# Scaling both halves of q on VectorE in the first seven pairs of a fused retention and WaveMLP kernel

## The chip, the cores and the metric

The kernel runs on one core of one Trainium2 chip. The metric is the device time of one execution in microseconds (us). The kernel before takes 168.33 us (median of 3 runs, 168.14 to 168.94). PE is TensorE, DVE is VectorE, ACT is ScalarE, POOL is GpSimd, SP is SyncE, which only issues transfers here. A run counts as slow when it lies more than 1.5% above the fastest run of its kernel; ratios use the other runs, called fast.

## The reference, cut to what matters

```python
# retention over q, k, v of shape (4, 8, 768, 64), fp32
for t in range(S):
    state = gamma * state + outer(k[:, :, t], v[:, :, t])
    y[:, :, t] = scale * (q[:, :, t] @ state)
x = y.transpose(0, 2, 1, 3).reshape(B, S, H * D)
# WaveMLP phase
theta = x @ w_theta
y = w_tok_r @ (x * cos(theta)) + w_tok_i @ (x * sin(theta))   # over tokens
u = x + y
out = u + relu(u @ w_ch)
```

The kernel works in blocks. It multiplies q by `scale * gamma**t` and v by `gamma**-t` per token and head; then the decay drops out of the products, and only a causal mask is left.

## The kernel before

The work goes in 12 "pairs" (three per batch), each with two 128-token blocks of q, k and v. A pair's q is 512 KB of fp32. `prep` scales it and casts it to bf16, in two halves of 128x512:

```python
def prep(n, name, engines):
    t = work.tile([P, 2, dm], BF, name="kqb", bufs=12)
    ...
    sc = qscp if name == "q" else vscp
    for two in range(2):
        engines[two].tensor_mul(dst[:, two], src[:, two],
                                _bcast_last(sc[:, 2 * g + two], D))
```

In pairs 0 to 6 `engines` for q is `DP = (DV, PL)`, one half on DVE and one on POOL; v is always on POOL (`PP`). Later pairs have both on POOL. TensorE then transposes the scaled q and k into a PSUM tile of the tag "tr" (two buffers), which DVE copies to SBUF:

```python
def flip(n, name, copy=nc.vector.tensor_copy):
    ps = psum.tile([P, 2, NP, P], BF, name="kq_ps", tag="tr", bufs=2)
    ... # eight nc.tensor.transpose
    copy(t, ps)
```

The same two buffers serve the transposes of the token weights (`w_ps`), of x (`x_ps`) and the channel product (`o_ps`), so each waits until DVE or ACT has emptied the tile before it (in pair 6 DVE's copy of x ended at 63.46 us and the transposes of q began at 63.50). `x_sb` is the copy of x's transposes, `z` is x times cos and sin, `at` is the masked block product. Pair 6's part of the program, on each engine in this order:

```python
# iteration n = 5, cut
ret_mask(n, 0)                       # DVE: at
prep(n + 1, "k", (PL,))              # POOL: k of pair 6
preps(DP)                            # q: DVE and POOL; v: POOL
...
theta(n - 1, 0); x_pe(n - 1)         # PE, then DVE: x_sb
theta(n - 1, 1)
flip(n + 1, "k"); flip(n + 1, "q")   # PE, then DVE: kqT
```

Of the kernel before, what the change touches and what calls it, by code (L numbers as in the profile page):

```python
# [21 lines left out]
def _bcast_last(ap: bass.AP, n: int) -> bass.AP:  # L22
    return bass.AP(tensor=ap.tensor, offset=ap.offset, ap=list(ap.ap) + [[0, n]])
# [9 lines left out]
def kernel(  # L33
# [42 lines left out]
    def load(n, name):  # L76

        b, g = divmod(n, nG)
        t = io.tile([P, H, 2 * D], FT, name="pair", bufs=7)
        src = dict(k=k, q=q, v=v)[name]  # L80
        nc.sync.dma_start(out=t, in_=src[b, :, 2 * g * P:2 * (g + 1) * P, :].rearrange(
            "h (p two) d -> p h (two d)", two=2))
        raw[n, name] = t
# [78 lines left out]
    def prep(n, name, engines):  # L162
        g = n % nG
        t = work.tile([P, 2, dm], BF, name="kqb", bufs=12)
        src = raw[n, name].rearrange("p h (two d) -> p two h d", two=2)
        dst = t.rearrange("p two (h d) -> p two h d", h=H)
        if name == "k":
            if engines[0] is nc.scalar:
                nc.scalar.copy(dst, src)
            else:  # L170
                engines[0].tensor_copy(dst, src)
        else:
# [4 lines that stand above are left out]
        st[n, name] = t  # L177
# [4 lines that stand above are left out]
            for j in range(NP):  # L182
                nc.tensor.transpose(ps[:, two, j, :],  # L183
                                    st[n, name][:, two, j * P:(j + 1) * P], ident)
        t = work.tile([P, 2, NP, P], BF, name="kqT", bufs=6)
        if copy:
            copy(t, ps)  # L187
        st[n, name + "T"], st[n, name + "_ps"] = t, ps

    def flip_out(n, name):  # L190
        nc.vector.tensor_copy(st[n, name + "T"], st[n, name + "_ps"])

    def flip_dma(n, name):
        t = work.tile([P, 2, NP, P], BF, name="kqT", bufs=6)
        nc.sync.dma_start_transpose(out=t.rearrange("p w j t -> p (w j) t"),
                                    in_=st[n, name].rearrange("p w d -> p (w d)"))
        st[n, name + "T"] = t
# [111 lines left out]
    def theta(n, a):  # L309
        th_ps = psum.tile([P, dm], FT, name="th_ps", tag="acc", bufs=2)  # L310
        for j in range(NP):
            nc.tensor.matmul(th_ps, st[n, "xT"][:, a, j, :], wth[:, j, :], start=(j == 0),  # L312
                             stop=(j == NP - 1))
        cs = work.tile([P, 2, dm], BF, name="cs", bufs=3)
        nc.scalar.activation(cs[:, 0, :], th_ps, AF.Sin, bias=halfpi, scale=1.0)  # L315
        nc.scalar.activation(cs[:, 1, :], th_ps, AF.Sin, bias=zerob, scale=1.0)  # L316
        st[n, "cs", a] = cs
# [32 lines left out]
    def moe_U_dma(m):  # L350
        uT = work.tile([P, nD, P], BF, name="uT", bufs=4)
        nc.sync.dma_start_transpose(out=uT, in_=mo[m]["u"])
        mo[m]["uT"] = uT
# [30 lines left out]
    def w_cast(t0):  # L384
        for r in range(2):
            row = work.tile([P, S], BF, name="wrow", bufs=5)
            nc.gpsimd.tensor_copy(row, wdma[r, t0])  # L387
            wrow[r, t0] = row
# [73 lines left out]
    def keep_busy(times):  # L462
        for _ in range(times):
            nc.tensor.matmul(warm_ps, warm[:, 0:P], warm, start=True, stop=True)


    DV, PL, AC = nc.vector, nc.gpsimd, nc.scalar
    DP, PP = (DV, PL), (PL, PL)
    keep_busy(12)
    prep(0, "k", (AC,))  # L470
    flip(0, "k", None)
    prep(0, "q", DP)
    flip_out(0, "k")
    keep_busy(3)
    flip(0, "q")
# [18 lines left out]
    ret_out(0, 0, DV.tensor_copy)  # L494
    ret_out(0, 1, DV.tensor_copy)
    keep_busy(3)
    prep(1, "q", DP)
    theta(0, 0)
    flip(1, "k")
    theta(0, 1)  # L500
# [22 lines left out]
    prep(2, "k", (PL,))  # L523
    zmul(0, 0)
    flip(2, "k")
    prep(2, "q", DP)
    theta(1, 0)
    zmul(0, 1)
    theta(1, 1)
# [26 lines left out]
    moe_M(0, 2, 3)  # L556
    theta(2, 0)
    flip(3, "k")
    prep(3, "q", DP)
    theta(2, 1)  # L560
    moe_M(0, 3, 4)
    x_pe(2)
# [29 lines left out]
    for n in range(nG, B * nG + 1):  # L592
        mine, done = tiles_of[n], tiles_of[n - 1]
        late, two = n > nG, len(mine) > 1
        nxt = n + 1 in pairs

        if nxt and n + 1 >= K_DMA:
            flip_dma(n + 1, "k")
        if nxt and n + 1 >= Q_DMA:
            flip_dma(n + 1, "q")  # L600
        if n <= X_DMA and n + 3 in pairs:
            load(n + 3, "k")
        if n >= U_DMA:
            moe_U_dma(done[1])
        def preps(engines):
            prep(n + 1, "q", engines)
            prep(n + 1, "v", PP)
            if n in (nG, nG + 1):
                w_cast(n - nG + 4)

        if n == nG:
            nc.gpsimd.tensor_copy(wch, wdma["ch"])
        if nG + 3 < n + 1 < Q_DMA:
            preps(PP)
        if late:
            ret_I(n - 1, 1)

        if n in pairs:
            ret_A(n, 0)
            ret_mask(n, 0)  # L620
        if n == nG:
            moe_M(0, 5, nT)
            w_flip(1, 2)
            moe_u(0)
            moe_M(1, 4, nT)
            moe_u(1)
        if late:
            ret_Y(n - 1, 1)
            ret_S(n - 1, 1)
            ret_out(n - 1, 0, nc.scalar.copy)  # L630
            ret_out(n - 1, 1, nc.scalar.copy)
            state_out(n - 1, 1)
            if n < nG + 3:
                prep(n + 1, "k", (PL,))
                if n > nG + 1:
                    preps(DP)
            if n - 1 >= X_DMA:
                x_dma(n - 1)
        if n > X_DMA and n + 3 in pairs:
            load(n + 3, "k")  # L640
        if n + 3 in pairs:
            load(n + 3, "q")

        first = mine[0]
        moe_M(first, 0, 3 if two else 2)
        if late:
            theta(n - 1, 0)
            if n - 1 < X_DMA:
                x_pe(n - 1)
            if n == nG + 1:  # L650
                preps(DP)
            theta(n - 1, 1)
        if two:
            moe_M(first, 3, nT)
            moe_u(first)
        for name, limit in (("k", K_DMA), ("q", Q_DMA)):
            if nxt and nG + 1 < n + 1 < limit and (n > nG + 1 or name == "k"):
                flip(n + 1, name)
        if n + 1 >= K_DMA and not two:
            moe_M(first, 2, 4)  # L660
        if n + 3 in pairs:
            load(n + 3, "v")
        for t in stores_in(n):
            store(t)
        if n + 1 >= U_DMA:
            moe_U_dma(first)

        if n in pairs:
            ret_S(n, 0)
            state_out(n, 0)  # L670
            ret_A(n, 1)
            ret_mask(n, 1)
            ret_Y(n, 0)
            ret_I(n, 0)
        if n < U_DMA:
            moe_U(done)
        if n == nG:
            prep(n + 1, "k", (AC,))
            preps(DP)
        if n == nG or n + 1 < K_DMA and not two:  # L680
            moe_M(first, 2, 4)
        early_z = late and n < nG + 3
        if early_z and n > nG + 1:
            zmul(n - 1, 0)
        if n < nG + 3:
            w_tok(n - nG + 3)
        if early_z:
            zmul(n - 1, 0 if n == nG + 1 else 1)
        if not two:
            moe_M(first, 4, nT)  # L690
            if n == nG + 1:
                flip(n + 1, "q")
            moe_u(first)
            if n == nG + 1:
                zmul(n - 1, 1)
        elif n in pairs:
            moe_M(mine[1], 0, nT)
        if n + 2 in pairs and n > nG + 1:
            prep(n + 2, "k", (AC,))
        if n + 2 in pairs and n + 2 >= Q_DMA:  # L700
            prep(n + 2, "q", PP)
            prep(n + 2, "v", PP)
        if two and n in pairs:
            moe_u(mine[1])
        for i, t in enumerate(done):
            if n == nG:
                flip(n + 1, "kq"[i])
            moe_O(t)
            moe_out(t)
        if late and not early_z:  # L710
            zmul(n - 1, 0)
            zmul(n - 1, 1)
        if n not in pairs:
            moe_M(mine[1], 0, nT)
            moe_u(mine[1])
# [43 lines left out]
```

## Time and profile before

| | busy us | share of the 166.5 us span |
|---|---|---|
| PE | 155.2 | 93% |
| DVE | 102.4 | 61% |
| ACT | 79.1 | 48% |
| POOL | 66.6 | 40% |

A busy share is an average over stages with different limits. From 70 us on TensorE hardly waits (it is busy for 9.84 of the 10 us from 70 to 80 and 31.74 of the 32 from 100 to 132); from 30 to 70 us its waits are short (38.30 of 40 us busy). So the views to read are the timelines of DVE and POOL up to 70 us and the chain of waits there.

### The profile page before, as it was taken

To read this page: it belongs to the slowest core of one execution; us is meant where nothing else is said; L and a number is where in the kernel's file an instruction comes from. 1 tells how busy PE (TensorE), PEld (TensorE's weight loads), DVE (VectorE), ACT (ScalarE), POOL (GpSimd) and SP (SyncE) were. 2 spreads that over 40 slices of the span, in tenths; PEclk is the share of its full clock that TensorE was granted. 3 is DMA by queue.
4 is the path that set the end of the run, shared out by engine and by line. 5 is a ranking of instruction groups with operands and counts; after the bars stand their busy time and mean duration, and the time that the engine had idled before them with its cause. 6 is when DMAs were issued, how large, how long until landed. Compare 5 with 4: busy or idle time off the path is not lost.

```text
span 166.5 us, 4614 instructions
## 1 busy us (share of the span) xinstructions
PE 155.2 (93%) x1933; PEld 87.2 (52%) x1959; DVE 102.4 (61%) x137; ACT 79.1 (48%) x137; POOL 66.6 (40%) x82
## 2 busy tenths in 40 slices
PE   6969897899999999999999999999999999999991
PEld 2345664664755667555555554455545444444460
DVE  2257798878686699939446464584554736334442
ACT  7216568371819467687847827447083350000010
POOL 6275959786685877771442703600000000000000
PEclk9999999999999999999999999999999999999999
DMA  4999999999999999999999999998996161753343
GB/s 122 309 345 307 326 326 354 286 328 317 293 311 349 277 278 331 309 202 250 206 231 298 163 242 203 195 233 168 266 145 185 32 189 32 231 115 100 106 141 135
DMA packets 68901, 38.45 MB, mean 231 GB/s; under 512 B 26256, under 2 KB 63376, under 8 KB 68880
## 3 DMA queue, kind: packets, MB, share of 16 engines
q1 hardware_dynamic: 68736, 38.02, 90.2%
q8 instruction: 15, 0.25, 0.7%
q10 hardware_dynamic: 144, 0.13, 0.2%
q14 instruction: 6, 0.05, 0.1%
HBM read 25.69 MB, written 6.29 MB: 192 GB/s over the span
## 4 chain that ended last, share of the span: by engine, by line
PE 77%; DVE 12%; DMA 3%; issue 3%; ACT 1%; POOL 1%; DVEq 0%; SPq 0%; POOLq 0%
PE y_ps L340 33%; PE o_ps L368 12%; PE th_ps L312 11%; PE at_ps L208 4%; PE yT_ps L231 4%; DVE at L215 4%; DMA pair<-in_q_dram 3%; PE yT_ps L245 3%; PE st_ps L262 3%; PE kq_ps L183 3%; DVE z L322 2%; PE w_ps L393 2%; DVE kqT L187 2%; PE y_ps L420 2%; DVE kqb L175 1%
## 5 line engine op out<-in xcount | busy, mean ns | idle before, releaser
L340 PE MATMUL y_ps<-z,wtr 128*128 128x512 bf16 x133 | 50.5, 379 | 1.1
L340 PE MATMUL y_ps<-z,wti 128*128 128x512 bf16 x122 | 46.2, 379 | 0.4 <-issue 0.2
L347 DVE TENSOR_TENSOR u<-y_ps,x_sb 128x512 bf16<-128x512 f32 x23 | 15.9, 690 | 27.0 <-PE y_ps L340 27.0
L215 DVE TENSOR_TENSOR at<-at_ps,maskp 128x1024 bf16<-128x1024 f32 x24 | 29.3, 1221 | 4.6 <-PE at_ps L208 4.6
L175 POOL TENSOR_TENSOR kqb<-pair,qscp 128x512 bf16<-128x512 f32 x17 | 19.3, 1150 | 28.9 <-DMA pair<-in_q_dram 26.0
L175 POOL TENSOR_TENSOR kqb<-pair,vscp 128x512 bf16<-128x512 f32 x24 | 26.6, 1131 | 5.0 <-DMA pair<-in_v_dram 4.9
L285 ACT CAST xT<-yT_ps 128x512 bf16<-128x512 f32 x20 | 13.5, 739 | 30.0 <-PE yT_ps L231 29.9
L375 DVE SCALAR_TENSOR_TENSOR ot<-o_ps,u 128x512 f32<-128x512 f32 x23 | 15.9, 690 | 13.2 <-PE o_ps L368 13.2
L312 PE MATMUL th_ps<-wth,xT 128*128 128x512 bf16 x93 | 23.2, 379 | 0.5 <-ACT xT L285 0.3
L368 PE MATMUL o_ps<-wch,uT 128*128 128x512 bf16 x92 | 22.8, 379 | 0.3
L340 PEld LDWEIGHTS <-wtr 128*128 128x128 bf16 x138 | 13.5, 98 | 13.8
L276 ACT CAST stbd<-st_ps 64x256 bf16<-64x256 f32 x40 | 14.7, 368 | 12.5 <-PE st_ps L262 12.0
L340 PEld LDWEIGHTS <-wti 128*128 128x128 bf16 x138 | 13.5, 98 | 13.6 <-ACT wti L400 0.4
L315 ACT ACTIVATE cs<-th_ps,halfpi 128x512 bf16<-128x512 f32 x24 | 16.5, 689 | 7.0 <-PE th_ps L312 6.6
L322 DVE TENSOR_TENSOR z<-cs,x_sb 128x1024 bf16<-128x1024 bf16 x24 | 18.8, 808 | 0.1
L316 ACT ACTIVATE cs<-th_ps,zerob 128x512 bf16<-128x512 f32 x24 | 16.5, 687 | 0.0
L312 PEld LDWEIGHTS <-xT 128*128 128x128 bf16 x96 | 8.9, 98 | 11.0 <-ACT xT L285 1.0
L368 PEld LDWEIGHTS <-uT 128*128 128x128 bf16 x92 | 8.8, 98 | 10.5 <-issue 0.6
L208 PE MATMUL at_ps<-kqT 64*64 64x128 bf16 x384 | 10.6, 221 | 2.6 <-DVE at L215 1.8
L430 ACT COPY uT<-u_ps 128x384 bf16<-128x384 bf16 (+1 forms) x2 | 0.7, 372 | 25.5 <-PE u_ps L429 25.5
L187 DVE COPY kqT<-kq_ps 128x1024 bf16<-128x1024 bf16 x14 | 9.6, 688 | 4.2 <-PE kq_ps L183 4.1
L387 POOL CAST wrow<-wtok 128x768 bf16<-128x768 f32 x12 | 10.5, 902 | 0.3 <-DMA wtok<-in_moe_w_tok_i_dram 0.2
(61 smaller groups left out, 164.4 us busy)
## 6 DMA issues: line engine op xcount, KB each, us to landing
pair<-in_k_dram SPq DMA_DIRECT2D x12, 512.0 KB, 6.7
pair<-in_q_dram SPq DMA_DIRECT2D x12, 512.0 KB, 7.7
pair<-in_v_dram SPq DMA_DIRECT2D x12, 512.0 KB, 8.2
out_dram<-ot SPq DMA_DIRECT2D x23, 256.0 KB, 2.6
wtok<-in_moe_w_tok_r_dram SPq DMA_DIRECT2D x6, 384.0 KB, 6.4
wtok<-in_moe_w_tok_i_dram SPq DMA_DIRECT2D x6, 384.0 KB, 5.8
w<-in_moe_w_theta_dram SPq DMA_DIRECT2D x1, 1024.0 KB, 8.3
w<-in_moe_w_ch_dram SPq DMA_DIRECT2D x1, 1024.0 KB, 8.5
```

The source lines that it names most:

```text
L175: engines[two].tensor_mul(dst[:, two], src[:, two], _bcast_last(sc[:, 2 * g + two], D))
L208: nc.tensor.matmul(at_ps[half, par, j, :], kT[rows, two, j, half], qT[rows, :, j, half], start=(j == 0), stop=(j == NP - 1), skip_group_ch ...
L215: nc.vector.tensor_mul(at.rearrange("p a j t -> p (a j) t"), at_ps.rearrange("p a j t -> p (a j) t"), _bcast_mid(maskp[:, two].rearrange(" ...
L276: nc.scalar.copy(stbd[(c + 1) % 2][sl, :, sl], st_ps[b][sl])
L312: nc.tensor.matmul(th_ps, st[n, "xT"][:, a, j, :], wth[:, j, :], start=(j == 0), stop=(j == NP - 1))
L315: nc.scalar.activation(cs[:, 0, :], th_ps, AF.Sin, bias=halfpi, scale=1.0)
L316: nc.scalar.activation(cs[:, 1, :], th_ps, AF.Sin, bias=zerob, scale=1.0)
L322: nc.vector.tensor_mul(zs[b][:, c], st[n, "cs", a], _bcast_mid(xs[b][:, c, :], 2))
L340: nc.tensor.matmul(y_ps, wT[r][:, s0, t0 * P:(t0 + 1) * P], zs[b][:, s0, r, :], start=(s0 == 0 and r == 0), stop=(s0 == nT - 1 and r == 1))
L347: nc.vector.tensor_add(u, mo[m]["y"], xs[b][:, t0, :])
L368: nc.tensor.matmul(o_ps, mo[m]["uT"][:, j, :], wch[:, j, :], start=(j == 0), stop=(j == nD - 1))
L375: nc.vector.scalar_tensor_tensor(ot, mo[m]["o"], 0.0, mo[m]["u"], ALU.max, ALU.add)
```

## The change

The intent is to take the slower engine out of q: POOL needs 1.04 us for a half, DVE 0.69, and each tensor of a pair then belongs to one engine.

```diff
-    DP, PP = (DV, PL), (PL, PL)
+    DD, PP = (DV, DV), (PL, PL)
...
-    prep(0, "q", DP)
+    prep(0, "q", DD)
... (the same for pairs 1, 2, 3)
-                    preps(DP)
+                    preps(DD)
... (the same at the two other places, pairs 4 and 5)
```

More of the change, by code (lines that the diff above doesn't have):

```diff
@@ L496 @@
     keep_busy(3)
-    prep(1, "q", DP)
+    prep(1, "q", DD)
     theta(0, 0)
@@ L525 @@
     flip(2, "k")
-    prep(2, "q", DP)
+    prep(2, "q", DD)
     theta(1, 0)
@@ L558 @@
     flip(3, "k")
-    prep(3, "q", DP)
+    prep(3, "q", DD)
     theta(2, 1)
@@ L650 @@
             if n == nG + 1:
-                preps(DP)
+                preps(DD)
             theta(n - 1, 1)
@@ L678 @@
             prep(n + 1, "k", (AC,))
-            preps(DP)
+            preps(DD)
         if n == nG or n + 1 < K_DMA and not two:
```

## The prediction

> **What bounds the kernel now.** I read the page's busy shares first, then the chain that ended last, then the timelines of VectorE (DVE) and GpSimd (POOL) in the first 70 us, where the changed instructions stand.
>
> ```profile
> span 166.5 us, 4614 instructions
> PE 155.2 (93%) x1933; PEld 87.2 (52%) x1959; DVE 102.4 (61%) x137; ACT 79.1 (48%) x137; POOL 66.6 (40%) x82
> PE 77%; DVE 12%; DMA 3%; issue 3%; ACT 1%; POOL 1%; DVEq 0%; SPq 0%; POOLq 0%
> ```
>
> TensorE is busy 93% of the span and is 77% of the chain, so the end moves only if TensorE waits more or less. DVE has 12% of the chain; POOL, from which the change takes work, has 1%. A table of engine busy time by stretches gives where the waits lie: TensorE works 9.84 of the 10 us from 70 to 80, 19.79 of the 20 us from 80 to 100 and 31.74 of the 32 us from 100 to 132. A delay made before 70 us is therefore not absorbed afterwards. From 30 to 70 us TensorE has 38.3 of 40 us, so little is hidden there either. Before 30 us both DMA arrivals and short chains between engines set the pace.
>
> The groups of instructions give the cost of one scaling of half a pair of q:
>
> ```profile
> L175 POOL TENSOR_TENSOR kqb<-pair,qscp 128x512 bf16<-128x512 f32 x17 | 19.3, 1150 | 28.9 <-DMA pair<-in_q_dram 26.0
> L175 DVE TENSOR_TENSOR kqb<-pair,qscp 128x512 bf16<-128x512 f32 x7 | 5.7, 813 | 5.5 <-DMA pair<-in_q_dram 5.5
> ```
>
> The means hide waiting: the view of the tile gives 1042/1044/1550 ns (least, median, most) on POOL and 668/691/1347 on DVE. Undisturbed, one takes 1.04 us on POOL and 0.69 on DVE, and DVE's next instruction starts 0.61 after it.
>
> [...] These are timelines of POOL and DVE about pair 6, then about pair 2:
>
> ```profile
> 61.26 2.49 POOL L175 TENSOR_TENSOR kqb<-pair,vscp 128x512 bf16<-128x512 f32 x2 [0.51 <-DMA pair<-in_v_dram]
> 61.50 1.35 DVE L175 TENSOR_TENSOR kqb<-pair,qscp 128x512 bf16<-128x512 f32 x1
> ...
> 24.33 0.93 DVE L175 TENSOR_TENSOR kqb<-pair,qscp 128x512 bf16<-128x512 f32 x1
> 25.14 2.49 POOL L175 TENSOR_TENSOR kqb<-pair,vscp 128x512 bf16<-128x512 f32 x2 [0.42 <-DMA pair<-in_v_dram]
> 25.19 1.54 DVE L322 TENSOR_TENSOR z<-cs,x_sb 128x1024 bf16<-128x1024 bf16 x1
> ```
>
> At 61.26 POOL begins the first half of v; DVE's q waits to about 62.30 and then needs 0.55, ending at 62.85; POOL's second half starts only then (1.04 + 0.41 waiting + 1.04 = 2.49). So the two take turns: at 62.30 POOL's own next instruction was ready, and DVE still got its turn; at 25.2 POOL, waiting since 25.14, came before DVE's next instruction z, which then took 1.54. [...]
>
> **The change, part by part.** Seven POOL instructions go (7 x 1.04 = 7.3 us of POOL time, plus its waits) and seven DVE instructions come (7 x 0.61 = 4.3 us of DVE time). The order of the other instructions on every engine is the same. POOL mostly gains nothing on the path: its next work, v, starts after "DMA pair<-in_v_dram" in most pairs. So the freed POOL time becomes idle time. What counts is where DVE's extra 0.61 falls, and whether it makes q take another turn behind v. By pair:
>
> Pair 0: q lands at 7.08. Now POOL's half waits for DVE's and ends at 8.67. With both on DVE the second ends near 8.37. DVE's following copy of k moves to 8.30–8.91, so the copy of q starts at 8.91 in place of 9.16: a gain of 0.25. It lasts until pair 2, whose k cast on POOL waits for DMA until 21.86.
>
> Pair 1: q lands at about 15.2, both halves end near 16.5; TensorE flips q at about 17, so no change.
>
> Pair 2: q halves at 24.1 and 24.7, ending 25.3. v lands at 25.14, so POOL goes next, to 26.35, and z ends at 26.9 in place of 26.7. I take +0.15 on the path.
>
> Pair 3: q begins near 34.43 (34.28 plus 0.15) and v lands at 34.52, in the middle of it. POOL takes the turn, 35.0 to 36.0, and the second q ends at 36.55. Then come the copy of x, 36.5 where it was 35.42, which frees the PSUM buffer for the flip of q, and z behind v's second half, to 38.1 where it was 37.4. That is about +0.65, up to +0.8 with the casts of w behind it.
>
> Pair 4: q lands at 44.09; DVE's copy of w (44.70 now) moves by 0.6 to 0.7, and TensorE's flip of k waits for it with no slack. This coincides with the delay there already: still about +0.8.
>
> Pair 5: DVE sits idle 1.23 us before the copy of w at 56.32, which takes up most of the extra: +0.
>
> Pair 6 decides, as the chain of waits by time shows:
>
> ```profile
> 60.45 1.13 DVE at L215
> 61.58 1.27 DVE kqb L175
> 62.85 0.61 DVE x_sb L306
> 63.46 0.04 issue
> 63.50 0.61 PE kq_ps L183 x8
> ```
>
> Here DVE itself is the path. The copy of x stands behind q on DVE, and TensorE's transposes of q wait for it. With two q instructions the turns are: v to 62.30, q to 62.85, v to 63.90, q to 64.45. If DVE comes later than 62.30 (by the +0.8), both halves of v go first and the second q ends at 64.45 again. So the copy of x starts at 64.45 in place of 62.8, 0.55 + 1.04 = 1.6 later, and the transposes at 65.1 in place of 63.5. The earlier +0.8 lies within these 1.6 and is not added.
>
> [...] TensorE waits for the copy of w behind it (67.44 to 67.97). The shifted order may win back about 0.2 of this. The sum is +1.6 - 0.2 = +1.4 us, to 168.33 + 1.4 = about 169.8.
>
> **The rivals.**
>
> 1. Taking POOL out of q ends the collisions within q and so gains. For it: q took 1.52 and 1.55 on POOL in pairs 0 and 1, with 0.5 of waiting; the two halves now run one after the other anyway (0.55 + 1.04 = 1.6 us, against 1.2 for two on DVE). Against it: only pair 0 has q on the path early enough; the later ones trade a collision of q with q for one of q with v. If the turns favour the engine that is already running, so that two DVE instructions go together, pair 6 costs only 0.6 and pairs 2 and 3 about nothing: 168.0 to 168.9.
>
> 2. The delays add up. If DVE reaches pair 3 some 0.1 us later than I say, POOL's first half of v goes before the first q: then q ends at 37.7 and the transposes of q start about 1.8 late. DVE would then meet v again in pair 4 (45.6), and the delay would come to 2.6 or 3.2 us: 171 to 171.5. The margin (34.43 against 34.52) is too thin to rule it out. Against it: [...] a late DVE finds pair 6's v already done.
>
> 3. The extra DVE time is hidden: DVE is only 61% busy, and 4.3 us more makes 64%. For it: pairs 1 and 5. Against it: the windows 60 to 65 and 65 to 70 have DVE busy 4.99 and 5.00 of 5 us. Fully hidden would mean 168.1 to 168.5.
>
> **Range and chances.** Rival 1 or 3 gives the low end; rival 2 the high end. Between the two the turns of pair 6 are the best supported, by the trace's own order of turns. I take 169.8, with 168.5 to 171.3. A change of 2% is 3.37 us: faster needs below 164.96, more than every gain listed together, so 0.01; slower needs above 171.70, only with rival 2 at its worst, so 0.07; within 2%: 0.92.
>
> **What would show it.** In the changed profile: POOL falls by 7 to 10 us, DVE rises by about 4 to 6 (waits count as busy); in pair 6 the two q instructions span about 2.9 us from 61.5 with v's second half between; the copy of x starts near 64.4 and the transposes of q near 65.1; every TensorE stretch after 70 us is the old one moved by 1.2 to 1.7 us. Wrong would be: the copy of x before 63.6 (turns not alternating), transposes of pair 3's q later than 37.8 (delays adding up), or a later stretch of TensorE that shrinks.

## The result, and the profile after

The first four runs of the changed kernel took 170.39, 174.55, 170.51 and 173.60 us; the second and fourth count as slow. A ratio in this text is the mean time of one kernel's fast runs over that of the other's of the same rounds, so it is not quite the ratio of the medians quoted. The ratio to before is 1.0118 (95% interval 1.0075 to 1.0161): within 2%, on the slow side. The predicted ratio was 169.8/168.33 = 1.0087.

From the page of the changed kernel (span, busy times, chain, the two groups of q):

```profile
span 168.7 us, 4613 instructions
PE 154.6 (92%) x1933; PEld 87.1 (52%) x1959; DVE 106.8 (63%) x144; ACT 79.1 (47%) x137; POOL 57.8 (34%) x75
PE 67%; DMA 11%; SPq 7%; DVE 7%; ACT 2%; issue 2%; POOL 1%; DVEq 0%
L175 POOL TENSOR_TENSOR kqb<-pair,qscp 128x512 bf16<-128x512 f32 x10 | 10.4, 1061 | 20.5 <-DMA pair<-in_q_dram 20.5
L175 DVE TENSOR_TENSOR kqb<-pair,qscp 128x512 bf16<-128x512 f32 x14 | 10.7, 803 | 5.4 <-DMA pair<-in_q_dram 5.3
```

POOL lost 8.8 us of busy time (66.6 to 57.8) and DVE gained 4.4. POOL's relief bought nothing: it became waiting for transfers (4.9 us for v's before, 23.2 after). TensorE's busy time did not grow (155.2 us before, 154.6 after), so the 2.2 us that the span grew are TensorE's waits. Pair 6, the timelines of POOL and DVE:

```profile
61.88 2.05 POOL L175 TENSOR_TENSOR kqb<-pair,vscp 128x512 bf16<-128x512 f32 x2 [1.82 <-DMA pair<-in_v_dram]
63.01 2.07 DVE L175 TENSOR_TENSOR kqb<-pair,qscp 128x512 bf16<-128x512 f32 x2
65.00 0.68 DVE L306 COPY x_sb<-x_ps 128x1024 bf16<-128x1024 bf16 x1
```

and the chain of waits there (start, us, what):

```profile
61.96 1.13 DVE at L215
63.09 1.99 DVE kqb L175 x2
65.08 0.61 DVE x_sb L306
65.69 0.04 issue
65.73 0.61 PE kq_ps L183 x8
```

The chain has the same members as before, but DVE came to q at 63.01 in place of 61.50. The first half of v ended near 62.92 and the second was already running, so both halves of q waited until about 63.9 and then took 1.1 to 1.2 us. The copy of x starts 2.23 us later than before and TensorE's transposes 2.23 later (65.73 against 63.50).

So DVE was 1.5 us late before pair 6. The beginning of that is at pair 2, again DVE and POOL:

```profile
24.37 1.28 DVE L175 TENSOR_TENSOR kqb<-pair,qscp 128x512 bf16<-128x512 f32 x2
25.27 2.73 POOL L175 TENSOR_TENSOR kqb<-pair,vscp 128x512 bf16<-128x512 f32 x2 [2.23 <-DMA pair<-in_v_dram]
25.57 1.53 DVE L322 TENSOR_TENSOR z<-cs,x_sb 128x1024 bf16<-128x1024 bf16 x1
```

The second half of q runs while v is waiting; v goes next, and z waits for it and ends at 27.1.

How late is TensorE after each step? The kernel before was profiled twice and the changed one three times (the further runs are told below). The table has the start of the same TensorE instructions (the last line: DVE's first output of the last tile) in the timelines, and in brackets the lateness against the mean of the two profiles of before.

| instruction | before, twice | after | after_again | after_third |
|---|---|---|---|---|
| products of pair 2 (at_ps) | 27.38, 27.27 | 27.76 (+0.43) | 27.73 (+0.40) | 27.84 (+0.51) |
| transposes of pair 3's q | 36.41, 36.32 | 37.06 (+0.69) | 36.77 (+0.40) | 36.88 (+0.51) |
| products of pair 3, second block | 41.73, 41.63 | 42.80 (+1.12) | 42.09 (+0.41) | 42.26 (+0.58) |
| transposes of pair 4's k | 45.30, 45.19 | 46.81 (+1.56) | 46.09 (+0.84) | 46.26 (+1.01) |
| transposes of pair 5's q | 57.32, 57.22 | 58.82 (+1.55) | 58.32 (+1.05) | 58.28 (+1.01) |
| products of pair 6 | 69.14, 68.61 | 71.12 (+2.24) | 69.98 (+1.10) | 70.23 (+1.35) |
| first output of the last tile | 162.81, 162.28 | 164.79 (+2.24) | 163.65 (+1.10) | 163.90 (+1.35) |

Three steps recur: about 0.4 to 0.5 us at pair 2, another 0.43 to 0.44 from pair 3's second block to pair 4's k, and 0.05 to 0.7 about pair 6. Pair 3 itself added 0.7 in the first profile and at most 0.1 in the others. The two profiles of before differ by 0.43 us in what passes at pair 6, so the last step is uncertain by some 0.2. After pair 6 nothing is lost or won back.

In pair 4 DVE's copy of the weights stands behind q, as predicted, but a second thing came with it. From the timelines of ACT, DVE and PE in the second profile of the changed kernel:

```profile
44.14 1.29 DVE L175 TENSOR_TENSOR kqb<-pair,qscp 128x512 bf16<-128x512 f32 x2 [0.29 <-DMA pair<-in_q_dram]
45.24 0.80 ACT L400 COPY wti<-w_ps 128x768 bf16<-128x768 bf16 x1
45.35 0.55 DVE L400 COPY wtr<-w_ps 128x768 bf16<-128x768 bf16 x1
46.09 0.61 PE L183 MATMUL kq_ps<-ident,kqb 128*128 128x128 bf16 x8 [0.29 <-ACT wti L400]
```

In the kernel before the transposes of k followed DVE's copy (44.70 to 45.25, transposes 45.30). In the changed one they waited for ACT's copy (46.04): the build gave them the other buffer of "tr", the one that ACT's copy empties. DVE's copy ended at 45.90, so I estimate from these times that without this exchange of buffers they could have started some 0.15 us earlier here, and DVE's later copy would have made the other 0.3 of the step.

All the profiles together put the step down to the exchange. From the products of pair 3's second block to these transposes 3.55 to 3.57 us pass in the six profiles of before, only6, early6_only, pp6 and pp36 (the runs are told below). They are 4.00 to 4.01 in the seven profiles of the kernels with more DVE work in pair 4: the changed one (three profiles), not6, memset_all, merged_all and merged_again. All seven show the wait for ACT's copy. (only01 has 4.21 without it: its q landed late, and the wait was for DVE's copy.) In merged_again DVE's copy had ended at 45.76, well before the transposes (DVE, ACT, PE), so there the exchange alone made the step:

```profile
45.21 0.55 DVE L403 COPY wtr<-w_ps 128x768 bf16<-128x768 bf16 x1
45.35 0.80 ACT L403 COPY wti<-w_ps 128x768 bf16<-128x768 bf16 x1
46.20 0.61 PE L186 MATMUL kq_ps<-ident,kqb 128*128 128x128 bf16 x8 [0.29 <-ACT wti L403]
```

No run changes the exchange and nothing else.

### The profile page after: what moved, and what is told of

It reads as the page before. It is cut to its first block, busy times and chain, and to the rows that moved or that the text cites. A ratio compares the mean times of both kernels' runs of the same rounds, so it can differ in the third digit from the quotient of the medians.

```text
span 168.7 us, 4613 instructions
## 1 busy us (share of the span) xinstructions
PE 154.6 (92%) x1933; PEld 87.1 (52%) x1959; DVE 106.8 (63%) x144; ACT 79.1 (47%) x137; POOL 57.8 (34%) x75
## 4 chain that ended last, share of the span: by engine, by line
PE 67%; DMA 11%; SPq 7%; DVE 7%; ACT 2%; issue 2%; POOL 1%; DVEq 0%
PE y_ps L340 32%; PE o_ps L368 12%; PE th_ps L312 8%; DMA pair<-in_q_dram 6%; SPq L81 5%; DMA pair<-in_k_dram 5%; PE yT_ps L231 3%; PE at_ps L208 2%; PE st_ps L262 2%; PE yT_ps L245 2%; DVE kqb L175 2%; PE kq_ps L183 2%; PE y_ps L420 2%; DVE z L322 1%; SPq L95 1%
## 5 line engine op out<-in xcount | busy, mean ns | idle before, releaser
L175 POOL TENSOR_TENSOR kqb<-pair,vscp 128x512 bf16<-128x512 f32 x24 | 26.7, 1135 | 23.9 <-DMA pair<-in_v_dram 23.2
L347 DVE TENSOR_TENSOR u<-y_ps,x_sb 128x512 bf16<-128x512 f32 x23 | 15.9, 690 | 26.9 <-PE y_ps L340 26.7
L312 PE MATMUL th_ps<-wth,xT 128*128 128x512 bf16 x93 | 23.2, 379 | 0.5 <-ACT xT L285 0.3
L175 POOL TENSOR_TENSOR kqb<-pair,qscp 128x512 bf16<-128x512 f32 x10 | 10.4, 1061 | 20.5 <-DMA pair<-in_q_dram 20.5
L175 DVE TENSOR_TENSOR kqb<-pair,qscp 128x512 bf16<-128x512 f32 x14 | 10.7, 803 | 5.4 <-DMA pair<-in_q_dram 5.3
L183 PE MATMUL kq_ps<-ident,kqb 128*128 128x128 bf16 x120 | 9.3, 219 | 3.0 <-DVE x_sb L306 0.8
```

What stands on the lines that cost most here:

```text
L175: engines[two].tensor_mul(dst[:, two], src[:, two], _bcast_last(sc[:, 2 * g + two], D))
L312: nc.tensor.matmul(th_ps, st[n, "xT"][:, a, j, :], wth[:, j, :], start=(j == 0), stop=(j == NP - 1))
L347: nc.vector.tensor_add(u, mo[m]["y"], xs[b][:, t0, :])
```

## The experiments

All runs gave the right result. "before" was timed in the same rounds. The first four ran on one chip, the next four and the last four likewise.

**before_again** is the kernel before, unchanged, for a second profile.

> The kernel before, profiled a second time, to see how far the landing of transfers differs between two executions. In the first profile q of pair 3 had landed by 32.99 us and its v at 34.52; in the changed kernel they landed at 35.11 and 36.84. If that is chance between executions, this second profile of the same kernel should show landings that differ by 1 us or more from the first; if it belongs to the change, they should agree within 0.3 us. Time about 168.4 us.

One run, 167.68 us. v of pair 3 began at 35.25 (34.52 in the first profile), k of pair 2 at 22.14 (21.86), and v and q of pair 6 had landed by 60.72 and 59.12 (61.26 and 59.36). So the landings of one kernel, that is the ends of its transfers, differ by 0.3 to 0.7 us between these two executions, less than the 1 us that I had named for chance but more than the 0.3 for none. Among the three profiles of the changed kernel v of pair 3, waited for each time, began at 35.36, 36.30 and 36.84: 1.5 us apart. What matters for the argument: which instructions of DVE and POOL meet differs from run to run. In this run z of pair 2 went before v (25.31, 0.68 us; in the first profile it took 1.54 behind v) and TensorE was not late. And at pair 6 TensorE did not wait for DVE (DVE, then PE):

```profile
62.23 0.68 DVE L306 COPY x_sb<-x_ps 128x1024 bf16<-128x1024 bf16 x1
62.72 1.06 PE L183 MATMUL kq_ps<-ident,kqb 128*128 128x128 bf16 x16
```

These are the transposes of k and q in one run; in the first profile they took 1.29 us from 62.81, with the wait for the copy of x in the middle. So the prediction's premise, that DVE is the path in pair 6, held in the first profile and not in this one.

**after_again** is the changed kernel, unchanged.

> The changed kernel again, profiled a second time. Fast runs at about 170.4 us, ratio 1.012. If the late landing of pair 3's q (35.11 us) was chance, it lands nearer 33 us now, DVE meets v in pair 3 in turns (second q ends near 36.5) and the delay of TensorE after pair 3 is still 0.7 to 1.1 us; if it belongs to the change, it lands near 35 again. In either case the copy of x of pair 6 starts 1.6 to 2.3 us later than 62.77 and TensorE stays 1.4 to 2.1 us late to the end.

Fast runs 169.22, 169.41, 169.74 and 170.59 us, two slow ones (173.07, 174.34), ratio 1.0079 (1.0040 to 1.0118). Pair 3's q began at 34.64 without a wait for its transfer, while it began at 35.11 in the first profile of the changed kernel and in not6 below, and at 35.05 in only01 below, whose pair 3 is as before. So the later landing doesn't need the edit of pair 3. Whether those of pairs 0 and 1 bring it is open: three of the seven profiles of kernels that have them show it, and none of the seven without (there POOL began pair 3's q by 33.63). Its cost does belong to the change. In only01, with a half of q on each engine, the copy of x began at 35.66 and TensorE was 0.1 us late after pair 3. In the first profile of the changed kernel the second half of q held that copy until 36.33, z then met v (37.11, 1.32 us), and TensorE lost 0.7. The halves of q of pair 3 ended near 35.9, not in turns with v. Pair 5 did take turns; POOL first, then DVE:

```profile
53.03 2.49 POOL L175 TENSOR_TENSOR kqb<-pair,vscp 128x512 bf16<-128x512 f32 x2 [2.05 <-DMA pair<-in_v_dram]
53.34 2.73 DVE L175 TENSOR_TENSOR kqb<-pair,qscp 128x512 bf16<-128x512 f32 x2
```

v to 54.07, q to 54.6, v to 55.5, q to 56.07: four halves, by turns, 2.73 us for a work of 1.29. It delayed TensorE by only 0.2 us, since DVE had idle time behind it (1.23 us before 56.32 in the first profile of before). (In the first profile pair 5 went q, v, q, v, from 54.05 to 56.18.) The copy of x of pair 6 started at 63.86, 1.1 us later than in the first profile of before, less than I had expected.

**only6** has the change in pair 6 alone.

```diff
                 if n > nG + 1:
-                    preps(DP)
+                    preps(DD)
```

> Only pair 6 has both halves of q on DVE. Turn-taking theory: v's first half to 62.3, first q to 62.85, v's second half to 63.9, second q to 64.45, so the copy of x starts near 64.4 in place of 62.8, and the kernel takes 1.2 to 1.6 us more: 169.5 to 170.0 us, ratio 1.007 to 1.010. Rival, only DVE's time counts (0.61): 168.9 to 169.0, ratio 1.003 to 1.004. Rival, the lateness of pairs 2 to 5 is what counts: 168.3, ratio 1.000.

Ratio 1.0051 (1.0019 to 1.0083), median 169.10 us; six fast runs. Its timelines of POOL and DVE:

```profile
60.70 2.52 POOL L175 TENSOR_TENSOR kqb<-pair,vscp 128x512 bf16<-128x512 f32 x2 [2.07 <-DMA pair<-in_v_dram]
61.64 2.13 DVE L175 TENSOR_TENSOR kqb<-pair,qscp 128x512 bf16<-128x512 f32 x2
63.69 0.68 DVE L306 COPY x_sb<-x_ps 128x1024 bf16<-128x1024 bf16 x1
```

The turns are as the prediction has them (v, q, v, q), but v landed 0.56 us earlier than in the profile that I had predicted from, so everything ends 0.6 to 0.7 earlier: the copy of x at 63.69 in place of 64.4. Pair 6's own share is therefore about 0.5%, or 0.9 us, between my two theories' numbers; the interval holds both. The rival that pairs 2 to 5 alone count falls.

**not6** has the change in all pairs but pair 6.

> Pairs 0 to 5 have both halves of q on DVE, pair 6 as before. Delays of pairs 2 to 5 alone: in the changed kernel's profile DVE and TensorE were 1.5 us late just before pair 6; a late DVE then finds v of pair 6 under way and the single q ends near 63.9 to 64.4. Theory: 1.0 to 1.6 us more, 169.4 to 170.0 us, ratio 1.006 to 1.010, so that neither part alone accounts for less than half of the whole, and the two do not add. Rival, the two add: only6 and not6 together make 2.1 us, so this one at 0.5 to 0.8 us, ratio 1.003 to 1.005.

Ratio 1.0061 (1.0026 to 1.0097); four fast runs (168.98 to 169.96), two slow (171.96, 172.02). Together the parts would make 1.0051 + 1.0061 - 1 = 1.0112; the intervals don't decide whether the two add, and the change gave 1.0079 to 1.0118. The trace gives a reason why they need not (POOL, then DVE):

```profile
62.26 2.04 POOL L175 TENSOR_TENSOR kqb<-pair,vscp 128x512 bf16<-128x512 f32 x2 [1.14 <-DVE ot L375]
63.32 1.53 DVE L175 TENSOR_TENSOR kqb<-pair,qscp 128x512 bf16<-128x512 f32 x1
```

DVE reached the single q of pair 6 at 63.32, late by the other pairs, and q took 1.53 us because v was under way until 64.3; two halves took 2.07 in the first profile of the changed kernel. This is one profile, of the slowest of the four fast runs, so it is an argument and no proof.

**memset_all** is the kernel before plus DVE time without SBUF inputs: a memset of 128x580 after DVE's half of q in each of the seven pairs.

```diff
+            if engines == DP:
+                nc.vector.memset(scratch, 0.0)
```

> The kernel before, with a memset of 0.61 us on DVE after its half of q in each of the seven pairs: the same DVE time as the change adds, [...] and POOL keeps its half of q. Rival, DVE's time alone explains the loss: as much as the change, ratio 1.008 to 1.012. Turn-taking theory: only the plain 0.61 us counts where DVE is on the path (pair 4's copy of w, pair 6's copy of x 0.6 later, near 63.4), and these do not add fully: ratio 1.003 to 1.006; in pairs 2, 3 and 5 no 1.04 us wait is added.

Ratio 1.0038 (1.0002 to 1.0074), 0.64 us, about two fifths of what the change costs; the intervals overlap. In its profile the memsets took 0.54 us each, a little less than the 0.61 they stand for, and took no turn: at pair 3 one ran from 35.26 to 35.80 while v's two halves took their plain 2.04 us from 35.17. But the run doesn't isolate DVE's plain time. Its pair 4 has the exchange of buffers too (the transposes of k at 45.91, after ACT's copy and before DVE's began at 46.08), and pair 4's q landed late (44.86). At pair 6 the memset cost about nothing: from pair 5's transposes of q to pair 6's products 11.47 us passed, against 11.82 and 11.39 in the profiles of before, 11.66 to 12.30 in those of the changed kernel and 12.36 in only6.

**merged_all** does each pair's q as one DVE instruction.

```diff
-            for two in range(2):
-                engines[two].tensor_mul(dst[:, two], src[:, two], ...)
+            if engines[0] is engines[1] and engines[0] is nc.vector:
+                nc.vector.tensor_mul(dst, src, _bcast_last(sc[:, 2 * g:2 * g + 2], D))
+            else: ... # as before
```

> The change with q of a pair as one DVE instruction of 128x1024 (about 1.22 us) in place of two of 128x512: the same work, one turn against v in place of two. Turn-taking theory: where DVE meets v under way (pairs 5 and 6) q waits for at most one half of v, so q of pair 6 ends within 2.3 us of its start and no half of v lies inside it; 0.3 to 0.8 us less than the change, ratio 1.003 to 1.007. Rival, the turns do not matter: as the change, 1.008 to 1.012.

Ratio 1.0036 (0.9998 to 1.0074). In pair 6 q stood between the halves of v and lost one turn only (its timelines, POOL and DVE):

```profile
61.28 3.02 POOL L178 TENSOR_TENSOR kqb<-pair,vscp 128x512 bf16<-128x512 f32 x2 [2.25 <-DMA pair<-in_v_dram]
61.89 1.51 DVE L175 TENSOR_TENSOR kqb<-pair,qscp 128x1024 bf16<-128x1024 f32 x1
```

v takes 3.02 us, because its second half waits for the whole of q, and q takes 1.51.

**early6_only** has the change in pair 6 alone, with q ahead of the mask on DVE.

```diff
+        if n == nG + 2:
+            prep(n + 1, "k", (PL,))
+            prep(n + 1, "q", DD)
         if n in pairs:
             ret_A(n, 0)
             ret_mask(n, 0)
...
-                prep(n + 1, "k", (PL,))
-                if n > nG + 1:
-                    preps(DP)
+                if n <= nG + 1:
+                    prep(n + 1, "k", (PL,))
+                else:
+                    prep(n + 1, "v", PP)
```

> Only pair 6 has both halves on DVE, as in only6, but they stand ahead of the mask of pair 5 on DVE (near 60.4 us, before pair 6's v lands near 61) and the cast of k stays ahead of them on POOL. Turn-taking theory: no half of v comes between, both end near 61.6 to 62.7, the copy of x starts where it did (62.8 or earlier), and the time is that of before: ratio 0.998 to 1.002, against 1.005 for only6. Rival, DVE's 0.61 us is lost wherever it stands: 1.003 to 1.005.

A miss: ratio 1.0030 (0.9989 to 1.0072), unclear against both expectations. In the profiled run v landed before q could start, and the turns came all the same (POOL, then DVE):

```profile
60.43 2.49 POOL L175 TENSOR_TENSOR kqb<-pair,vscp 128x512 bf16<-128x512 f32 x2 [2.48 <-DMA pair<-in_v_dram]
60.81 2.66 DVE L175 TENSOR_TENSOR kqb<-pair,qscp 128x512 bf16<-128x512 f32 x2
63.39 1.21 DVE L215 TENSOR_TENSOR at<-at_ps,maskp 128x1024 bf16<-128x1024 f32 x1
```

A margin of some 0.6 us (60.4 against 61) to a transfer is less than landings vary here (v of pair 6 landed at 60.43 in this run and at 61.88 in the first profile of the changed kernel), so the run says nothing on whether an early q without v would be free. It is a third place with the turns v, q, v, q, in 2.66 us.

**only01** has the change in pairs 0 and 1 alone (`prep(0, "q", DD)`, `prep(1, "q", DD)`).

> Only pairs 0 and 1 have both halves on DVE. The prediction gave pair 0 a gain of 0.25 us (copy of q's transposes near 8.75 in place of 9.0 to 9.2), which is lost again at pair 2, whose k lands near 22. Expect the early gain in the trace and no change in time: ratio 0.998 to 1.001. If the gain lasted, 0.9985 or lower.

Ratio 1.0009 (0.9967 to 1.0051): no change. In the trace TensorE's first product of pair 0 starts at 9.48 against 9.90 in the first profile of before (of which 0.15 is an earlier landing), and at pair 2's transposes of k, 23.13 against 22.96 and 23.24, nothing of it is left.

**after_third** and **merged_again** are the changed kernel and merged_all, head to head.

> The changed kernel a third time, on the chip and in the rounds of merged_again. So far its ratio was 1.0118 and 1.0079. Expect 1.007 to 1.012, and in the trace of pair 5 or pair 6 a half of v between the two halves of q where DVE reaches q while v is under way (two q instructions together longer than 2 us).

> The change with q as one DVE instruction of 128x1024, head to head with after_third. Turn-taking theory: one turn less in pairs 5 and 6, 0.4 to 0.9 us less than after_third, ratio 1.003 to 1.006 (it was 1.0036). Rival, merged_all was low by chance: equal to after_third within 0.2 us.

after_third: five fast runs, 169.51 to 170.50 us, one slow (174.50), ratio 1.0099 (1.0060 to 1.0138). Neither pair 5 nor pair 6 had v between its halves of q, so that part of the expectation missed: in pair 5 both ran before v (53.51 to 54.8, v from 54.09), in pair 6 DVE came at 62.46, and both waited for v's end at 63.04. merged_again: 1.0074 (1.0043 to 1.0105), 0.3 us less than after_third on the means of the fast runs (169.65 against 169.97); the intervals overlap, and both the 0.4 to 0.9 us of the theory and the 0.2 of the rival are missed. In its pair 6 q came at 62.53, again with the second half of v already begun, and waited to 63.5. So the single instruction saves a turn where DVE comes between v's halves, as in merged_all; that it makes the kernel faster than the change is not settled.

**pp6** is the opposite of the change, in pair 6: both halves of q on POOL.

```diff
                 if n > nG + 1:
-                    preps(DP)
+                    preps(PP)
```

> The opposite of the change in pair 6 alone: both halves of q on POOL, none on DVE. If DVE is the path there and POOL has time, the copy of x starts as soon as its transposes are done (near 62.1 in place of 62.8), TensorE's transposes of q follow without a wait (63.25 in place of 63.5), and the time falls by 0.2 to 0.5 us: ratio 0.997 to 0.999. If v, now 1.0 us later on POOL, takes the path: 1.000 to 1.003.

Ratio 0.9983 (0.9947 to 1.0018), median 168.05 us against 168.47 of before: unclear in time. From its timelines (DVE, then PE):

```profile
61.99 0.69 DVE L306 COPY x_sb<-x_ps 128x1024 bf16<-128x1024 bf16 x1 [0.24 <-PE x_ps L299]
...
62.66 1.06 PE L183 MATMUL kq_ps<-ident,kqb 128*128 128x128 bf16 x16
```

The copy of x now waits for TensorE and not the other way round, and TensorE's sixteen transposes run without a break. But so they did in before_again and only01, in 1.06 us too, with a half of q on DVE: pp6 can win at TensorE only what the first profile of before lost there (11.82 us at pair 6, by the measure under memset_all, against 11.39 in before_again and in pp6). It is the fastest kernel by its median, within the noise of before.

**pp36** does the same in pairs 3 and 6.

> Pairs 3 and 6 with both halves of q on POOL. Pair 3's q lands at 33 to 35 us and DVE's copy of x and z behind it are on the path there; without q on DVE z comes 0.2 to 0.5 us earlier, unless q late on POOL (two halves end near 35.1 to 37.2) holds TensorE's transposes at 36.4: ratio 0.996 to 0.999 if the theory holds and q lands near 33, about 1.000 to 1.003 if POOL's two halves take the path.

Ratio 1.0002 (0.9967 to 1.0038). In pair 3 POOL had both halves by 35.06 in the profiled run, z began at 36.15 as before, and nothing was won. No version clearly beats the kernel before.

## Why the prediction was right

The measured fast runs, 170.39 and 170.51 us and then ratios of 1.0079 and 1.0099, lie in the range of 168.5 to 171.3. That DVE waits behind v, at pairs 2 and 6, is what the traces show: in the first profile z took 1.53 us at pair 2 (0.68 without v) and the two halves of q 2.07 at pair 6 (1.29 without v). Why an instruction of one engine holds up one of the other is not shown by any run. That the sum of 1.4 us came out is partly luck, since its parts differ: pairs 2 and 4 cost more than predicted, pair 3 cost nothing in two of three profiles, pair 6 alone cost 0.9 us (only6) and not 1.6, and the exchange of buffers was not foreseen. Of its signs, the busy times came true. But in none of the three profiles did v's second half lie between the two q of pair 6, and TensorE's stretches after it moved by 1.10 to 2.24 us, not by 1.2 to 1.7. Point by point:

- **POOL's time is not on the path: right.** POOL fell by 8.8 us and its waits for v's transfers grew, from 4.9 to 23.2 us in the list of waits.
- **Pair 0 gains 0.25, lost at pair 2: right**, by only01.
- **Pair 2, +0.15: mis-sized.** It measured 0.40 to 0.51. I let the early gain carry q to 24.1, but DVE's copy of k's transposes, which stands ahead of q, could not start before 23.76: q began at 24.37 in the first profile (24.35 and 24.45 in the others). z behind v then ended at 27.1 in place of my 26.9.
- **Pair 3 meets v in the middle: not seen.** In none of the three profiles did v come between the halves there (v began at 36.84, 35.36 and 36.30, when q was done or in its second half). It cost nothing in two profiles; in the first, where q landed late, pair 3 cost 0.7 us.
- **Pair 4 only coincides with an older delay: wrong.** It added 0.43 to 0.44 us in all three profiles, and TensorE's flip of k waited for ACT's copy of w in the exchanged buffer, not for DVE's; the sum, 0.84 and 1.01 in two profiles, is near the 0.8 predicted, and 1.56 in the first.
- **Pair 5 hidden: right**, 0 to 0.2 us, even with four halves in turns.
- **Pair 6 decides, and earlier delays are not added: half right.** TensorE was late by 1.01 to 1.55 us before pair 6, not by 0.8, and pair 6 added 0.05 to 0.7. The chain runs through q, the copy of x and the transposes in the changed kernel as predicted; the copy of x started at 65.00, 63.86 and 64.11 against the predicted 64.45, the transposes at 65.73, 64.59 and 64.84 against 65.1. The branch taken was mostly the one for a late DVE: v's second half had begun, so q waited for the end of v. Turns in the predicted order are shown by only6. That the earlier pairs and pair 6 do not add is argued from not6, whose single q took 0.85 us longer behind v than alone, and not shown.
- **After 66 us 0.2 comes back: right.** From the end of the transposes of pair 6 to its products 4.78 us pass in all three profiles, against 5.03 in the first profile of before (4.83 in the second); z takes 0.90 to 0.99 there in place of 1.54 (65.91 to 67.44, behind POOL's q of pair 7).

The rivals: that taking POOL out of q gains (1) falls, as every measured ratio is above 1. The snowball (2) is half true: delays did build up to 1.01 to 1.55 us before pair 6, but pair 6 then added only 0.05 to 0.7. Hidden DVE time (3) falls by the same ratios, and by only6, whose interval lies above 1; how much of the loss is DVE's plain time beside the waits for v and the exchange stays open, since memset_all has the exchange too.

One thing stays open. Of 16 runs of the changed kernel 5 were slow (173.1 to 174.6 us), of 6 runs of not6 2, of the 37 runs of the kernel before 2, and of the other kernels' none. The granted clock was 0.985 to 0.99 in four of the five, but 0.999 in the fifth and 1.0 in not6's two, and a run of before at 1.0 was slow too: it doesn't explain them all. No slow run left a trace. Whether a late transfer sets off more of the turns in such a run can't be told from these records, and nothing above rests on them.

## What to carry to other kernels

Moving work from POOL to DVE didn't end the collisions here, it changed who is met: in only6 the two halves of q met v and took 2.13 us, 1.29 without v. Ask at which time the moved instruction will reach the head of its queue and what the other engine will be doing then, and don't take work from an engine only because its instructions are longer: here POOL's relief of 8.8 us bought nothing, as POOL had 1% of the chain of waits. (Relieving DVE instead, in pp6 and pp36, gave no clear gain: ratios of 0.9983 and 1.0002.) Compare what releases each wait before and after: the same edit can change which PSUM buffer the build gives to a later tile (here, in pair 4, the transposes of k followed ACT's copy, which ended at 46.04 in after_again, in place of DVE's, at 45.25 in the kernel before). Where two engines meet by the landing of transfers, profile one kernel more than once before trusting a margin under a microsecond: one landing lay 1.5 us apart among three profiles of the changed kernel.

## What the runs measured of meetings and landings

- A half of q that takes 0.69 us on DVE alone took up to 1.55 when POOL's instruction had begun first (before_again, pair 1: POOL's q from 15.04, DVE's from 15.08). When both engines had more instructions queued, the one that waited mostly came next: q took its turns with v in 2.73 us (after_again, pair 5), 2.13 (only6) and 2.66 (early6_only). In after_third, pair 5, it did not: v began at 54.09, when the second half of q was due at 54.12 (53.51 and the pace of 0.61), and both halves still went through in 1.28 us.
- One meeting: a half of q or a z behind one POOL instruction of 1.04 us took up to 0.87 us longer (z 0.68 alone and 1.53 behind v, q 0.68 and 1.55).
- POOL against DVE, at 512 elements a partition: 1.04/0.69 = 1.5 by one instruction's duration, and 1.00/0.61 = 1.6 by the pace of two in a row (2.04 us on POOL, 1.29 on DVE).
- Landings between executions of one kernel: 0.3 to 0.7 us apart between two profiles of the kernel before, and 1.5 us for v of pair 3 among three of the changed kernel.
